# Scores of a slot's query chunks as one TensorE task, and smaller bookings in the ordering pass

## The chip, the cores and the metric

The kernel runs on one core of one Trainium2 chip. The metric is the device time of one execution in microseconds (us). An execution of the kernel before takes 1092.42 us (median of 3 runs).

## What is computed

Four batches of eight heads, 576 tokens, 64 dimensions each: causal softmax attention mixed with a linear memory read-out, and behind it two feed-forward layers on the 2304 x 512 result. All is float32.

```python
scores = where(causal, -1e9, q @ k.T / 8);  a = softmax(scores)
local  = a @ v
q_p    = where(q > 0, q, exp(q) - 1) + 1
mem    = (q_p @ M_prev) / (q_p @ z_prev + 1e-6)
x      = g * mem + (1 - g) * local            # g = sigmoid(beta), by head
h      = x @ moe_w_in;   x = (h * tanh(softplus(h))) @ moe_w_out
h      = x @ moe2_w_in;  out = (h * cos(h)) @ moe2_w_out
```

## The kernel before

**Attention.** `pair(m)` (L346) handles two heads of one batch; there are 16 pairs. It loads q, k, v, transposes q and k on TensorE (`prep`, L387: `f_tr` issues two or three transposes into one PSUM buffer, tiles ptq and ptk, and `f_ev` copies them to qT and kT). The 576 queries are five chunks, 0 of 64 rows and 1 to 4 of 128. They are dealt to three slots, `SLOTS = ((3, 0), (4,), (2, 1))`: slots 0 and 2 hold two chunks, slot 1 holds one. For each chunk `slot(x)` (L460) issues

- `f_sc` (L484): the scores of both heads into the slot's PSUM tile s (L491, two matmuls of 64 rows each), and the causal mask added by bf16 matmuls of pick and mask (L495); for chunk 4 also `f_sx` (L499, tile sx);
- `f_mx` (L513): the negated row maximum on VectorE (tile nm, L516), one column pair of nm for each chunk of the slot;
- `f_ex` (L528): the exponentials on ScalarE, one for each head, which read s and nm and write p (L532);
- `f_ph` (L544): the memory columns of p; and for the whole slot the sums and `f_sl` (L567), which scales p on VectorE (L569).

`flip` (L588) transposes p on TensorE (L584, tile t) and copies the blocks to PT; `pv` (L635) multiplies PT with v and M_prev (L651), the result goes through xs to DRAM.

**First feed-forward layer, first half.** `block0(bi)` (L718) takes 256 tokens at a time as soon as the four pairs of their batch are in DRAM: x is loaded and split in two float parts (x <- x, L731), `f_1` (L750, matmul line L756, tile h) and `f_2` (L791, matmul line L799, tile acc) are tasks of six matmuls. There are 9 such blocks, 1728 matmuls, and they lie between and behind the attention work. The weights are decoded on VectorE and ScalarE by `decode_w` (tiles dec and w, L125 to L142). The second half of the layer and the second layer (`late`, L884, L964, L966) follow.

**What sets the order.** All of this is first only booked: `add(engine, cost, function, deps, rank, takes, uses)` notes a task with a cost in us. `arrange()` (L176) then plays the tasks on a clock of its own: an engine that is free takes the ready task of lowest rank and is busy for the booked cost, buffers come free when all their users have ended, and TensorE is charged `SWITCH` when the mode of its tiles changes. The result is one list, and `run` issues the instructions in that order; each engine executes its own instructions in exactly that order. The booked costs therefore set the order alone. Where TensorE finds nothing ready before the first block0 task and its booked work of the last moments is too little, `arrange` inserts a dummy matmul (L303, tile warm) booked with 0.12 us (L250 to L260).

In the list as issued, a task's waits follow from what tiles its instructions read and write in the order of the list. So a matmul that writes s behind an instruction that reads s waits for that reader.

Of the kernel before, what the change touches and what calls it, by code (L numbers as in the profile page):

```python
# [10 lines left out]
F32 = mybir.dt.float32  # L11
# [18 lines left out]
def tile_kernel(ctx: ExitStack, tc: tile.TileContext, q, k, v, M_prev, z_prev, beta,  # L30
                moe_w_in, moe_w_out, moe2_w_in, moe2_w_out, out):
    nc = tc.nc
    B, H, S, D = q.shape
    NT, DM = out.shape
    DFF = moe_w_in.shape[1]
    P = 128
# [60 lines left out]
    pools = {}  # L97
# [243 lines left out]
    def misc(name):  # L341
        return pools["misc"].tile([P, 512], F32, tag="m", name=name)
# [3 lines left out]
    def pair(m):  # L346
# [40 lines left out]
        def prep(key, x):  # L387
            group = (QG if key == "q" else KG)[x]
            at = (0, 320 if key == "q" else 288)[x]
            w = sum(r for c, r in group)  # L390
            bm = Buf("misc")
            s = {}

            def f_tr(e):
                s["ps"] = ps = misc(f"pt{key}{m}_{x}")
                o = 0
                for c, r in group:
                    nc.tensor.transpose(ps[:, o:o + r], d[key][0:r, c].rearrange("p h d -> p (h d)"), ident[0:r, 0:r])  # L398
                    o += r

            def f_ev(e):
                if x == 0:
                    d[key + "T"] = A2.tile([P, S], F32, tag=f"{key}T", name=f"{key}T{m}")
                copy(e, d[key + "T"][:, at:at + w], s["ps"][:, 0:w], 0.125 if key == "q" else None)


            def f_kd(e):
                t = d["kd"] = kd[m % 2]
                for j in range(2):
                    copy(e, t[j * D:(j + 1) * D, j], s["ps"][j * D:(j + 1) * D, 512 - at:S - at])  # L410

            T_ = B_[key + "T"]
            takes = [bm] + ([T_] if x == 0 else []) + ([B_["kd"]] if key == "k" and x else [])
            tr = add("pe", 0.11 * len(group) + 0.05, f_tr, [dk if key == "k" else dq], R + 6, takes, [B_[key]])
            ev = add("act/dve", c_both(w), f_ev, [tr], R + 6, [], [bm, T_])
            got[key, x] = [ev]
            if key == "k" and x == 1:
                got[key, x].append(add("act/dve", (0.5, 0.4), f_kd, [tr], R + 6, [], [bm, B_["kd"]]))
# [41 lines left out]
        def slot(x):  # L460
# [1 line left out]
            bx = Buf("misc") if 4 in SLOTS[x] else None  # L462
            s = {"sp": {}}
            S_ = R + 20 + 10 * x
            at = 0
            def f_pt():
                if "pt" in s:
                    return
# [5 lines left out]
                    d["p", i_] = t[:, o:o + 2 * n_ + P].rearrange("p (h c) -> p h c", h=2)  # L474
                    o += 2 * n_ + P

            maxes, exps, cols = [], {}, {}
            t_m = fst = None
            for c, i in enumerate(SLOTS[x]):
                s0, nk = START[i], START[i] + ROWS[i]  # L480
                main = min(nk, 512)


                def f_sc(e, c=c, i=i, s0=s0, nk=nk, main=main, at=at):  # L484
                    if c == 0:
                        s["sc"] = pools["sc"].tile([P, 2, 512], F32, tag="s", name=f"s{m}_{x}")
                    o = s["sp"][i] = s["sc"][:, :, at:at + main]
                    qT, kT = d["qT"], d["kT"]
                    for j in range(2):
                        pr = slice(j * D, (j + 1) * D)  # L490
                        nc.tensor.matmul(o[:, j], qT[pr, s0:s0 + P], kT[pr, 0:main], start=True, stop=False)  # L491
                    for y in range(2 if i else 1):
                        for j in range(2):
                            pr = slice(j * D, (j + 1) * D)
                            nc.tensor.matmul(o[:, j, s0:main], pick[pr, y], mask[pr, y, 0:main - s0],  # L495
                                             start=False, stop=y == 1 or i == 0)


                def f_sx(e, s0=s0):  # L499
                    f_pt()  # L500
                    s["sx"] = o = misc(f"sx{m}")[:, 0:P]
                    nc.tensor.matmul(o, d["qT"][:, s0:s0 + P], d["kd"].rearrange("p j c -> p (j c)"), start=True, stop=False)
                    nc.tensor.matmul(o, ident_b, mask2.rearrange("p j c -> p (j c)"), start=False, stop=True)

                qd = [*got["q", 0 if i < 3 else 1]]
                kx = [*got["k", 0], *(got["k", 1] if nk > SH else ())]
                t_s = add("pe", main * 4 / 2400 + 0.35, f_sc, qd + kx + maxes[-1:], S_, [bs] if c == 0 else [],
                          [B_["qT"], B_["kT"]] + ([] if c == 0 else [bs]), mode=1)
                maxes.append(t_s)
                if nk > 512:  # L510
                    t_x = add("pe", 0.35, f_sx, qd + kx + maxes[-1:], S_, [bx, bp], [B_["qT"], B_["kd"]])

                def f_mx(e, c=c, i=i):  # L513
                    if c == 0:
                        s["nm"] = A2.tile([P, 2, 2], F32, tag="nm", name=f"nm{m}_{x}")
                    nc.vector.tensor_reduce(out=s["nm"][:, c], in_=s["sp"][i], axis=AX.X, op=ALU.max, negate=True)  # L516

                def f_mxx(e):
                    nm = s["nm"]
                    nc.vector.tensor_reduce(out=nm[:, 1], in_=s["sx"].rearrange("p (j c) -> p j c", j=2), axis=AX.X,  # L520
                                            op=ALU.max, negate=True)
                    nc.vector.tensor_tensor(out=nm[:, 0], in0=nm[:, 0], in1=nm[:, 1], op=ALU.min)

                t_m = add("dve", c_dve(2 * main), f_mx, [t_s, t_m], S_ + 1, [bn] if c == 0 else [], [bs] if c == 0 else [bs, bn])
                if nk > 512:
                    t_m = add("dve", 0.45, f_mxx, [t_m, t_x], S_ + 1, [], [bx, bn])

                def f_ex(e, j, part, c=c, i=i, main=main, nk=nk):  # L528
                    f_pt()
                    lo, hi = ((0, main), (main, nk))[part]  # L530
                    src = s["sp"][i][:, j] if part == 0 else s["sx"][:, j * HD:(j + 1) * HD]
                    nc.scalar.activation(d["p", i][:, j, D + lo:D + hi], src, AF.Exp, bias=s["nm"][:, c, j:j + 1], scale=1.0,  # L532
                                         accum_out=s["sm"][:, 1 if part else c, j:j + 1])

                for part in range(2 if nk > 512 else 1):
                    for j in range(2):
                        w = (main, nk - main)[part]
                        takes = [] if fst or bx else [bp]
                        t_e = add("act", 0.48 + 0.00083 * w, lambda e, j=j, part=part, f=f_ex: f(e, j, part), [t_m, fst], S_ + 2,
                                  takes, [bn] + ([] if takes else [bp]) + [bs if part == 0 else bx], func="exp")  # L540
                        exps[i, j, part] = t_e
                        fst = fst or t_e

                def f_ph(e, i=i):  # L544
                    nc.vector.tensor_tensor(out=d["p", i][:, :, 0:D], in0=d["ph"][:, i],  # L545
                                            in1=d["den"][:, i].unsqueeze(2).broadcast_to([P, 2, D]), op=ALU.mult)

                cols[i] = add("dve", 0.27, f_ph, [p4, fst], S_ + 3, [], [bp, B_["ph"], bden])
                at += nk

            def f_sm(e):
                sm = s["sm"]
# [35 lines left out]
        def flip(i, blocks, dst, x):  # L588
            nonlocal f0
            bm = Buf("misc")  # L590
            s = {}
            n = sum(ROWS[i_] for i_, h, j in blocks)

            def f_t(e):
                s["ps"] = ps = misc(f"t{m}_{i}")
                o = 0
                for i_, h, j in blocks:
                    tr(ps, o, i_, h, j)
                    o += ROWS[i_]

            def f_e(e):
                if "PT" not in d:
                    d["PT"] = A1.tile([P, 30, P], F32, tag="PT", name=f"PT{m}")
                o = dst(d["PT"])
                src = s["ps"][:, 0:n]
                if len(o.shape) == 3:
                    src = src.rearrange("p (a c) -> p a c", c=o.shape[2])
                copy(e, o, src)

            S_ = R + 25 + 10 * x  # L610
            t_t = add("pe", 0.115 * len(blocks) + 0.05, f_t, [f0] + [z_ for i_, h, j in blocks for z_ in (scaled[i_, h], colsof[i_])],
                      S_, [bm] + ([] if f0 else [B_["PT"]]), [ptof[i_] for i_, h, j in blocks])
            f0 = f0 or t_t
            t_e = add("act/dve", c_both(n), f_e, [t_t], S_ + 1, [], [bm, B_["PT"]])
            for i_, h, j in blocks:
                flipped.setdefault(i_, []).append(t_e)
# [510 lines left out]
```

## Time and profile before

| | us |
|---|---|
| time, median of 3 runs (lowest, highest) | 1092.42 (1090.91, 1093.68) |
| the profiled execution: its own time | 1091.78 |
| the profiled execution: span of its instructions | 1090.0 |
| TensorE (PE) busy | 1056.5 |
| VectorE (DVE) busy | 761.1 |
| ScalarE (ACT) busy | 570.6 |

The profile is one execution of the program. Its own time is 1.78 us longer than the span of its instructions. A group of instructions is named by its line, its engine, its operation, and the tiles it writes and reads (`nm<-s`). Idle time is that of the engine just ahead of the instruction, with what released it. Busy time of TensorE counts overlapping matmuls once, while the mean of one instruction is its full duration, so the time that one of a series costs is busy time divided by their number.

### The profile page before, as it was taken

Reading aid. Unit: us, or ns where it says so; the run is one execution under the profiler, and the core shown is the slowest. Engines: PE = TensorE matmul, PEld = TensorE weight load, DVE = VectorE, ACT = ScalarE, POOL = GpSimd, SP = SyncE. Lnnn points to the kernel's source line nnn. Section 1 sums busy time; section 2 is a strip of 40 time slices with the busy share of each in tenths; the row PEclk is TensorE's granted clock in tenths of the full one; section 3 lists DMA queues with packets and bytes.
Section 4 is the critical chain, followed back from the end, with each engine's and each line's share of the span. In section 5 each row is a group of like instructions: output and inputs, shape, how many; then the busy total and the mean of one; then the engine's idle time right before and its main releaser. Section 6 shows DMA issues by size and latency. Waiting matters only on the chain.

```text
span 1090.0 us, 17872 instructions
## 1 busy us (share of the span) xinstructions
PE 1056.5 (97%) x6907; PEld 937.7 (86%) x6907; DVE 761.1 (70%) x1699; ACT 570.6 (52%) x1272; POOL 3.9 (0%) x19
## 2 busy tenths in 40 slices
PE   7888999999999999999999999999999999999998
PEld 5555777877877899989999999999999999999997
DVE  6999997878768577537562218887667676666664
ACT  4666676756665433333323224766555455555544
POOL 1000000000000000000000000000000000000000
PEclk9999999999999999999999999999999999999999
DMA  6456322422230445306452215311000010000000
GB/s 158 108 150 170 92 64 67 120 65 59 69 105 25 161 146 161 120 25 205 166 184 87 72 44 174 117 39 59 1 29 30 1 59 1 29 30 1 30 1 29
DMA packets 112852, 88.71 MB, mean 81 GB/s; under 512 B 65792, under 2 KB 103680, under 8 KB 112768
## 3 DMA queue, kind: packets, MB, share of 16 engines
q1 hardware_dynamic: 112768, 87.58, 26.9%
q8 instruction: 54, 0.88, 0.3%
q14 instruction: 30, 0.25, 0.1%
HBM read 68.69 MB, written 18.87 MB: 80 GB/s over the span
## 4 chain that ended last, share of the span: by engine, by line
PE 85%; DVE 10%; ACT 3%; issue 1%; POOL 0%; ACTq 0%; POOLq 0%
PE h L884 28%; PE acc L966 18%; PE acc L964 9%; PE h L756 9%; PE acc L799 8%; PE pv L651 4%; PE t L584 4%; DVE nm L516 3%; PE s L491 3%; DVE p L569 2%; ACT p L532 1%; PE ptq L398 1%; DVE PT L317 1%; PE warm L303 1%; DVE p L545 1%
## 5 line engine op out<-in xcount | busy, mean ns | idle before, releaser
L884 PE MATMUL h<-x,w 128*128 128x384 f32 x1728 | 345.0, 337 | 1.6 <-ACT g L900 1.6
L884 PEld LDWEIGHTS h<-x,w 128*128 128x128 f32 x1728 | 307.3, 188 | 17.2 <-ACT g L900 1.8
L966 PE MATMUL acc<-w,G 128*128 128x512 f32 x864 | 228.4, 393 | 0.0
L966 PEld LDWEIGHTS acc<-w,G 128*128 128x128 f32 x864 | 159.9, 188 | 22.1
L951 DVE TENSOR_TENSOR G<-g,G 128x384 fp32r<-128x384 f32 x144 | 79.7, 555 | 100.1 <-ACT G L315 99.5
L756 PE MATMUL h<-x,w 128*128 128x256 f32 x864 | 128.9, 288 | 2.7 <-ACT g L315 1.6
L799 PE MATMUL acc<-G,w 128*128 128x256 f32 x864 | 129.9, 289 | 1.0 <-ACT o L315 0.7
L756 PEld LDWEIGHTS h<-x,w 128*128 128x128 f32 x864 | 111.6, 190 | 6.9 <-ACT g L315 4.5
L315 ACT ACTIVATE G<-g 128x384 fp32r<-128x384 f32 (+1 forms) x153 | 81.9, 535 | 66.3 <-DVE g L935 35.5
L799 PEld LDWEIGHTS acc<-G,w 128*128 128x128 f32 x864 | 112.2, 190 | 3.8 <-ACT o L315 1.9
L964 PE MATMUL acc<-G,w 128*128 128x384 f32 x576 | 112.6, 336 | 0.0
L532 ACT ACTIVATE p<-s,nm 128x448 f32<-128x448 f32 (+4 forms) x160 | 81.4, 517 | 43.7 <-DVE nm L516 16.4
L964 PEld LDWEIGHTS acc<-G,w 128*128 128x128 f32 x576 | 100.9, 188 | 0.0
L584 PE MATMUL t<-ident,p 128*128 128x128 f32 (+1 forms) x480 | 74.1, 280 | 10.5 <-DVE PT L317 6.3
L928 ACT ACTIVATE n<-n 128x384 f32<-128x384 f32 x96 | 49.9, 521 | 63.8 <-DVE n L924 63.8
L900 ACT ACTIVATE g<-h 128x384 f32<-128x384 f32 x48 | 23.5, 492 | 113.6 <-PE h L884 112.7
L516 DVE TENSOR_REDUCE nm<-s 128x2 f32<-128x128 f32 (+4 forms) x80 | 62.4, 793 | 21.8 <-PE s L495 11.2
L912 DVE TENSOR_SCALAR u<-hs 128x384 f32<-128x384 f32 x96 | 34.5, 359 | 54.6 <-ACT hs L315 51.9
L935 DVE TENSOR_TENSOR g<-n,hs 128x384 f32<-128x384 f32 x96 | 53.2, 555 | 26.3 <-ACT n L931 26.2
L584 PEld LDWEIGHTS t<-ident,p 128*128 128x128 f32 (+1 forms) x480 | 53.3, 142 | 21.2 <-DVE PT L317 8.8
L491 PE MATMUL s<-kT,qT 64*128 64x512 f32 (+4 forms) x320 | 61.8, 472 | 9.6 <-DVE nm L516 5.9
L315 ACT ACTIVATE hs<-h 128x384 f32<-128x384 f32 x96 | 47.1, 490 | 39.2 <-PE h L884 36.5
(91 smaller groups left out, 1216.4 us busy)
## 6 DMA issues: line engine op xcount, KB each, us to landing
raw<-in_moe_w_in_dram SPq DMA_DIRECT2D x32, 512.0 KB, 4.3
raw<-in_moe_w_out_dram SPq DMA_DIRECT2D x32, 512.0 KB, 4.0
k<-in_k_dram SPq DMA_DIRECT2D x32, 144.0 KB, 2.8
x1d<-xs SPq DMA_DIRECT2D x32, 144.0 KB, 2.0
xad<-o SPq DMA_DIRECT2D x9, 512.0 KB, 3.0
x2d<-o SPq DMA_DIRECT2D x6, 768.0 KB, 3.2
x<-x2d SPq DMA_DIRECT2D x6, 768.0 KB, 4.3
out_dram<-o SPq DMA_DIRECT2D x18, 256.0 KB, 2.0
```

The costliest lines, as they stand in the source:

```text
L315: nc.scalar.activation(dst, src, AF.Copy, scale=1.0 if scale is None else scale)
L491: nc.tensor.matmul(o[:, j], qT[pr, s0:s0 + P], kT[pr, 0:main], start=True, stop=False)
L516: nc.vector.tensor_reduce(out=s["nm"][:, c], in_=s["sp"][i], axis=AX.X, op=ALU.max, negate=True)
L532: nc.scalar.activation(d["p", i][:, j, D + lo:D + hi], src, AF.Exp, bias=s["nm"][:, c, j:j + 1], scale=1.0, accum_out=s["sm"][:, 1 if part ...
L584: nc.tensor.transpose(ps[:, at:at + r], d["p", i][0:r, h, j * P:(j + 1) * P], ident[0:r, 0:r])
L756: nc.tensor.matmul(h[:, half // 2], w[:, a, 0, c * P:(c + 1) * P], x[:, e_, c, :], start=c == 0 and pi == 0, stop=c == NKC - 1 and pi == 2)
L799: nc.tensor.matmul(t[:, c], w[:, a, 1, n * P:(n + 1) * P], G[:, e_, half], start=f == 0 and pi == 0 and c == 0, stop=f == NFH - 1 and pi == 2,
L884: nc.tensor.matmul(q_["h"], w[:, a, 0, c * P:(c + 1) * P], x[:, e_, c, :], start=c == 0 and pi == 0, stop=c == NKC - 1 and pi == 2)
L935: nc.vector.tensor_tensor(out=q_["g"], in0=q_["n"], in1=q_["hs"], op=ALU.mult)
L951: ENG[e].tensor_tensor(out=q_["G"][:, 1], in0=q_["g"], in1=q_["G"][:, 0].bitcast(F32), op=ALU.subtract)
L964: nc.tensor.matmul(o, w[:, a, 1, c * P:(c + 1) * P], G[:, e_, :], start=st, stop=sp_)
L966: nc.tensor.matmul(o, G[:, a, c * P:(c + 1) * P], w[:, e_, 1, :], start=st, stop=sp_)
```

## The change

`f_sc` moves out of the loop over the slot's chunks: it issues the scores and masks of all chunks of the slot behind each other, and is one task. It waits for both halves of kT and for every half of qT that its chunks need. Its booking is `main * 4 / 2400 + 0.15` for each chunk, where each chunk was a task of its own with `main * 4 / 2400 + 0.35`. The bookings of the transposes shrink: of q and k from `0.11 * n + 0.05` to `0.1 * n + 0.02`, of p from `0.115 * n + 0.05` to `0.109 * n + 0.02`. The second transpose task of q or k depends on the first one, and the tiles qT and kT are allocated with the first transposes instead of with the first copy.

```diff
             def f_tr(e):
+                if x == 0:
+                    d[key + "T"] = A2.tile([P, S], F32, tag=f"{key}T", name=f"{key}T{m}")
                 s["ps"] = ps = misc(f"pt{key}{m}_{x}")
...
-            tr = add("pe", 0.11 * len(group) + 0.05, f_tr, [dk if key == "k" else dq], R + 6, takes, [B_[key]])
+            tr = add("pe", 0.1 * len(group) + 0.02, f_tr, [dk if key == "k" else dq, *got.get((key, "tr"), ())], R + 6, takes, [B_[key]])
+            got[key, "tr"] = [tr]
...
-                def f_sc(e, c=c, i=i, s0=s0, nk=nk, main=main, at=at):
-                    if c == 0:
-                        s["sc"] = pools["sc"].tile([P, 2, 512], F32, tag="s", name=f"s{m}_{x}")
+            def f_sc(e):
+                s["sc"] = pools["sc"].tile([P, 2, 512], F32, tag="s", name=f"s{m}_{x}")
+                qT, kT = d["qT"], d["kT"]
+                at = 0
+                for i in SLOTS[x]:
+                    s0, main = START[i], min(START[i] + ROWS[i], 512)
                     o = s["sp"][i] = s["sc"][:, :, at:at + main]
...
+            t_s = add("pe", sum(min(START[i] + ROWS[i], 512) * 4 / 2400 + 0.15 for i in SLOTS[x]), f_sc, qd + kx, S_, [bs],
+                      [B_["qT"], B_["kT"]], mode=1)
...
-                t_s = add("pe", main * 4 / 2400 + 0.35, f_sc, qd + kx + maxes[-1:], S_, [bs] if c == 0 else [],
-                          [B_["qT"], B_["kT"]] + ([] if c == 0 else [bs]), mode=1)
-                maxes.append(t_s)
                 if nk > 512:
-                    t_x = add("pe", 0.35, f_sx, qd + kx + maxes[-1:], S_, [bx, bp], [B_["qT"], B_["kd"]])
+                    t_x = add("pe", 0.35, f_sx, [*qd, *kx, t_s], S_, [bx, bp], [B_["qT"], B_["kd"]])
...
-            t_t = add("pe", 0.115 * len(blocks) + 0.05, f_t, [f0] + [z_ for i_, h, j in blocks for z_ in (scaled[i_, h], colsof[i_])],
+            t_t = add("pe", 0.109 * len(blocks) + 0.02, f_t, [f0] + [z_ for i_, h, j in blocks for z_ in (scaled[i_, h], colsof[i_])],
```

How the change moves instructions, at three places. In tile names the first number is the pair and the second the slot or the part; most lines of the changed program stand three to nine lines further down.

**TensorE, slot 2 of pair 14, where block0 tasks fill the engine.** Before (the bf16 weight loads and masks are left out):

```order
L799 MATMUL acc0_3_0_3994<-G0_3_3_4295,w0_6_1744 128x256 x6
L756 MATMUL h0_4_1_4388<-x4_3711,w0_2_1001 128x256 x6
L491 MATMUL s14_2_4415<-kT14_4050,qT14_4191 128x320 x2
...
L799 MATMUL acc0_3_0_3994<-G0_3_3_4295,w0_7_1919 128x256 x6
L491 MATMUL s14_2_4415<-kT14_4050,qT14_4191 128x192 x2
...
L584 MATMUL t14_3_4445<-ident_85,p14_0_4337 128x128 x4
```

Now:

```order
L759 MATMUL h0_4_1_4175<-x4_3886,w0_3_1262 128x256 x6
L491 MATMUL s14_2_4501<-kT14_4081,qT14_4282 128x320 x2
...
L491 MATMUL s14_2_4501<-kT14_4081,qT14_4282 128x192 x2
...
L587 MATMUL t14_3_4521<-ident_85,p14_0_4456 128x128 x4
L759 MATMUL h0_4_2_4530<-x4_3886,w0_4_1445 128x256 x12
```

The scores of the second chunk (192 columns) stood behind another task and now follow those of the first (320 columns) with only their masks between.

**TensorE, the end of pair 4 and the first block0 matmuls (h0_0_0).** Before (dummies left out where the dots are):

```order
L584 MATMUL t4_4_1456<-ident_85,p4_1_1336 128x128 x4
L584 MATMUL t4_4_1464<-ident_85,p4_1_1336 128x128 x4
...
L584 MATMUL t4_4_1478<-ident_85,p4_1_1336 128x128 x2
L756 MATMUL h0_0_0_1482<-x0_1325,w0_0_452 128x256 x6
```

Now:

```order
L587 MATMUL t4_4_1487<-ident_85,p4_1_1317 128x128 x4
L587 MATMUL t4_4_1494<-ident_85,p4_1_1317 128x128 x4
L587 MATMUL t4_4_1505<-ident_85,p4_1_1317 128x128 x2
L587 MATMUL t4_2_1511<-ident_85,p4_2_1424 128x128 x3
L587 MATMUL t4_2_1516<-ident_85,p4_2_1424 128x128 x3
...
L759 MATMUL h0_0_0_1536<-x0_1373,w0_0_444 128x256 x6
L587 MATMUL t4_1_1546<-ident_85,p4_2_1424 128x128 x2
```

Six transposes of slot 2 (t4_2), and further up the first transposes of q of pair 5 and of k of pair 6, now stand ahead of the first block0 matmul: 12 more transposes in all. The dummies ahead of it are 218 instead of 187.

**VectorE, the row maxima of slots 0 and 1 of pair 4.** Before:

```order
L128 SCALAR_TENSOR_TENSOR dec0_4_1_1257<-raw0_4_1_1063,dec0_4_1_1257 128x512
L516 TENSOR_REDUCE nm4_0_1318<-s4_0_1296 128x2
L516 TENSOR_REDUCE nm4_1_1331<-s4_1_1311 128x2
L516 TENSOR_REDUCE nm4_0_1318<-s4_0_1296 128x2
L545 TENSOR_TENSOR p4_0_1333<-ph4_1259,den4_1292 128x2x64 x2
```

Now:

```order
L520 TENSOR_REDUCE nm4_0_1306<-s4_0_1183 128x2
L142 TENSOR_TENSOR w0_3_1262<-dec0_3_1_1241,w0_3_1262 128x512
L438 TENSOR_TENSOR mn4_1271<-ph4_1300,z4_1020 128x640
L520 TENSOR_REDUCE nm4_0_1306<-s4_0_1183 128x2
L444 TENSOR_REDUCE den4_1336<-mn4_1271 128x10
```

Between the two maxima of slot 0 stood one instruction and now stand two. The second one still comes behind exponentials of the first chunk: it writes the tile nm which they read, and waits for the last of them that is ahead of it in the list, before for that of the first head, now for that of the second.

**Counts over the whole order.** From the first block0 matmul to the last one TensorE changes between the modes of its tiles (scores; p times V; all else) 112 times before and 96 times now. Ahead of the last matmul of the attention stand 834 of the 1728 block0 matmuls before and 942 now. Ahead of the first split of x on VectorE (x <- x, L731) there are now three decode steps, three copies to PT and two copies to kT fewer, and two copies to qT, four to kd, four scalings of p, two small sums and one copy to xs more.

## Rows read from the trace of the kernel before

**Rows 1.** The page: busy time of the engines.

```profile
PE 1056.5 (97%) x6907; PEld 937.7 (86%) x6907; DVE 761.1 (70%) x1699; ACT 570.6 (52%) x1272; POOL 3.9 (0%) x19
```

**Rows 2.** Busy time by stretch: from, to, length, engines, clock, DMA.

```profile
0.00:107.00 107.00, 89.72 (x720) 61.67 (x721) 93.82 (x246) 63.92 (x200) 3.87 (x19) 0.98 0.56 145
107.00:360.00 253.00, 244.37 (x2052) 196.54 (x2052) 206.69 (x540) 165.74 (x445) 0.00 (x0) 1.00 0.29 74
360.00:500.00 140.00, 135.95 (x1060) 130.97 (x1059) 84.57 (x153) 55.00 (x86) 0.00 (x0) 1.00 0.44 142
500.00:1090.00 590.00, 586.48 (x3081) 548.55 (x3079) 376.05 (x764) 285.97 (x542) 0.00 (x0) 1.00 0.17 59
```

**Rows 3.** Timeline of TensorE around the first matmul of block0.

```profile
106.88 0.44 PE L584 MATMUL t<-ident,p 128*128 128x128 f32 x2
107.07 0.96 PE L756 MATMUL h<-x,w 128*128 128x256 f32 x6
```

**Rows 4.** Waits of TensorE from 107 to 360 us: total, times, longest.

```profile
PE s L491 <- DVE nm L516: 4.5, 8, 1.6
PE s L491 <- ACT p L532: 1.1, 3, 0.5
PE ptk L398 <- DVE kT L317: 0.8, 1, 0.8
PE h L756 <- DVE g L317: 0.8, 1, 0.8
```

**Rows 5.** TensorE groups by form from 107 to 360 us, the scores.

```profile
L491 PE MATMUL s<-kT,qT 64*128 64x192 f32 x44 | 6.6, 375 | 3.4 <-DVE nm L516 2.5 <-ACT p L532 0.8
L491 PE MATMUL s<-kT,qT 64*128 64x64 f32 x44 | 4.8, 295 | 2.5 <-DVE nm L516 2.0 <-ACT p L532 0.4
```

**Rows 6.** TensorE groups from 0 to 107 us: dummies and transposes.

```profile
L303 PE MATMUL warm<-zeros,ident_b 128*128 128x256 bf16 x187 | 28.5, 293 | 2.0 <-DVE zeros L300 2.0
L584 PE MATMUL t<-ident,p 128*128 128x128 f32 (+1 forms) x139 | 23.3, 293 | 9.8 <-DVE PT L317 6.0 <-ACT PT L315 2.0 <-ACT kd L315 1.5
```

**Rows 7.** VectorE groups by form, whole span: those of the count.

```profile
L131 DVE SCALAR_TENSOR_TENSOR dec<-raw,dec 128x512 int32<-128x512 int32 x64 | 43.9, 687 | 1.0
L317 DVE COPY PT<-t 128x512 f32<-128x512 f32 x32 | 21.8, 684 | 1.1 <-PE t L584 0.8
L569 DVE TENSOR_SCALAR p<-p,sm 128x320 f32<-128x320 f32 x32 | 11.0, 380 | 0.1
L319 DVE TENSOR_SCALAR qT<-ptq 128x320 f32<-128x320 f32 x5 | 2.4, 482 | 0.1
L317 DVE COPY kd<-ptk 64x64 f32<-64x64 f32 x12 | 2.6, 217 | 0.1
```

**Rows 8.** Waits of VectorE from 20 to 107 us: total, times, longest.

```profile
DVE nm L516 <- ACT p L532: 1.3, 3, 0.9
DVE nm L516 <- PE s L495: 0.5, 2, 0.3
```

**Rows 9.** The same from 107 to 360 us.

```profile
DVE nm L516 <- ACT p L532: 8.2, 10, 2.0
```

**Rows 10.** Timeline of TensorE, scores of slots 0 and 1, and slot 2.

```profile
113.30 0.44 PE L491 MATMUL s<-kT,qT 64*128 64x64 f32 x4 [0.73 <-DVE nm L516]
...
113.60 1.11 PE L491 MATMUL s<-kT,qT 64*128 64x512 f32 x4
...
121.13 0.60 PE L491 MATMUL s<-kT,qT 64*128 64x192 f32 x4
...
121.77 2.41 PE L756 MATMUL h<-x,w 128*128 128x256 f32 x18
```

**Rows 11.** L799 alone by form: first 140 to 360 us, then 380 to 480 us.

```profile
L799 PE MATMUL acc<-G,w 128*128 128x256 f32 x354 | 56.1, 294 | 0.0
L799 PE MATMUL acc<-G,w 128*128 128x256 f32 x389 | 57.2, 284 | 0.4 <-DVE G L776 0.4
```

More of the change, by code (lines that the diff above doesn't have):

```diff
@@ L401, in f_ev @@
             def f_ev(e):
-                if x == 0:
-                    d[key + "T"] = A2.tile([P, S], F32, tag=f"{key}T", name=f"{key}T{m}")
                 copy(e, d[key + "T"][:, at:at + w], s["ps"][:, 0:w], 0.125 if key == "q" else None)
@@ L464, in slot @@
             S_ = R + 20 + 10 * x
-            at = 0
             def f_pt():
@@ L475, in f_pt @@
                     o += 2 * n_ + P
-            maxes, exps, cols = [], {}, {}
+            exps, cols = {}, {}
             t_m = fst = None
-            for c, i in enumerate(SLOTS[x]):
-                s0, nk = START[i], START[i] + ROWS[i]
-                main = min(nk, 512)
-                def f_sc(e, c=c, i=i, s0=s0, nk=nk, main=main, at=at):
-                    if c == 0:
-                        s["sc"] = pools["sc"].tile([P, 2, 512], F32, tag="s", name=f"s{m}_{x}")
+            def f_sc(e):
[4 more added lines that the diff above has]
+                    s0, main = START[i], min(START[i] + ROWS[i], 512)
                     o = s["sp"][i] = s["sc"][:, :, at:at + main]
-                    qT, kT = d["qT"], d["kT"]
                     for j in range(2):
@@ L496, in f_sc @@
                                              start=False, stop=y == 1 or i == 0)
+                    at += main
+            qd = [t_ for y in sorted({0 if i < 3 else 1 for i in SLOTS[x]}) for t_ in got["q", y]]
+            kx = [*got["k", 0], *got["k", 1]]
+            t_s = add("pe", sum(min(START[i] + ROWS[i], 512) * 4 / 2400 + 0.15 for i in SLOTS[x]), f_sc, qd + kx, S_, [bs],
+                      [B_["qT"], B_["kT"]], mode=1)
+            for c, i in enumerate(SLOTS[x]):
+                s0, nk = START[i], START[i] + ROWS[i]
+                main = min(nk, 512)
                 def f_sx(e, s0=s0):
@@ L503, in f_sx @@
                     nc.tensor.matmul(o, ident_b, mask2.rearrange("p j c -> p (j c)"), start=False, stop=True)
-                qd = [*got["q", 0 if i < 3 else 1]]
-                kx = [*got["k", 0], *(got["k", 1] if nk > SH else ())]
-                t_s = add("pe", main * 4 / 2400 + 0.35, f_sc, qd + kx + maxes[-1:], S_, [bs] if c == 0 else [],
-                          [B_["qT"], B_["kT"]] + ([] if c == 0 else [bs]), mode=1)
-                maxes.append(t_s)
                 if nk > 512:
-                    t_x = add("pe", 0.35, f_sx, qd + kx + maxes[-1:], S_, [bx, bp], [B_["qT"], B_["kd"]])
+                    t_x = add("pe", 0.35, f_sx, [*qd, *kx, t_s], S_, [bx, bp], [B_["qT"], B_["kd"]])
                 def f_mx(e, c=c, i=i):
@@ L548, in slot @@
                 cols[i] = add("dve", 0.27, f_ph, [p4, fst], S_ + 3, [], [bp, B_["ph"], bden])
-                at += nk
             def f_sm(e):
```

## The prediction

> **What bounds the kernel now.** I read the page first, then the busy time by stretch, then the waits inside the stretches that have idle time. TensorE is busy for 1056.5 of 1090.0 us [rows 1], so no other engine can be the bound over the whole span; but 28.5 us of that are dummies [rows 6]. Useful work of TensorE is 1056.5 - 28.5 = 1028 us, and the span is this plus dummies plus idle time. The stretches say where these lie [rows 2]. Up to 107 us TensorE is busy for 89.7 us, dummies among them, so 61.2 us are useful and 45.8 us are lost; VectorE is busy for 93.8 of the same 107 us. This start is bound by VectorE, and it ends with the first matmul of block0 at 107.07 us [rows 3], from which on TensorE always has feed-forward work beside the attention. From 107 to 360 us TensorE idles for 253.0 - 244.4 = 8.6 us, from 360 to 500 us for 4.0 us, and behind that for 3.5 us in 590 [rows 2]. So a change to the order can win in two ways only: by more useful matmuls in the start or a shorter start, and by less waiting behind it. From 500 us on there is nothing to win.
>
> Of the 8.6 us, 4.5 are scores that wait for the row maximum on VectorE and 1.1 are scores that wait for the exponentials on ScalarE [rows 4]. The forms name them: all of it lies ahead of the scores of 192 and of 64 columns [rows 5], which are the second chunks of slots 2 and 0. They write the tile s behind an instruction that reads its first part, and wait for that reader.
>
> **The change part by part.** The sum is made against the profiled execution's own time, 1091.78 us, which lies 0.64 below the median of 1092.42.
>
> *The wait of second chunks.* Now nothing reads s between the two chunks, so the wait goes by construction. TensorE bounds the time behind 107 us, so I count it all: 11 waits, **-5.6** [rows 4]. The same waits ahead of 107 us cost nothing, since TensorE has dummies and idle time there.
>
> *The transposes.* Twelve more stand ahead of the first block0 matmul. One costs 23.3 us / 139 = 0.168 us [rows 6], together **-2.0**: they fill time that is lost today, and are gone from the full stretch. The 31 further dummies lie in the same lost time and cost nothing as long as VectorE is the later engine there; if it weren't, they would cost 31 x 28.5/187 = 4.7 us [rows 6].
>
> *VectorE ahead of the first split of x.* Three decode steps and three copies to PT fewer at 0.68 to 0.69 us each, and two copies to kT that I price like the copy to qT, are -5.1 us. Two copies to qT at 0.48, four to kd at 0.22, four scalings at 0.38 and a copy to xs at about 0.5 are +3.9, two small sums some +0.2 [rows 7]. So the work of the engine that bounds the start hardly changes: **-1.0**.
>
> *The second maximum of a slot.* It waits for an exponential of the first chunk, since both touch nm. Now it often stands closer to the first maximum and waits for the exponential of the second head. In the start VectorE lost 1.3 us to that in 3 waits, 0.9 the longest [rows 8]. There are ten such places ahead of the first block0 matmul (five pairs, two slots). The bounds of what is added are 0 and 10 x 0.9 - 1.3 = 7.7; I take as much again as there is now, **+1.3**, as only 3 of 10 showed at all.
>
> *The first maximum of a slot.* It now waits for the scores of both chunks. A second chunk takes 113.60 - 113.30 = 0.30 us in slot 0 and 121.77 - 121.13 = 0.64 in slot 2 [rows 10], so five pairs give at most 5 x 0.94 = 4.7 us in the start, and at least 0. VectorE waited for scores for only 0.5 us from 20 to 107 us [rows 8]: it is usually late for them. I take **+0.5**. Behind 107 us VectorE has 253.0 - 206.7 = 46 us to spare [rows 2], and the delay is hidden as long as TensorE doesn't come to wait for VectorE in turn.
>
> *Mode changes.* There are 16 fewer. A block0 matmul costs 56.1/354 = 0.158 us between attention work and 57.2/389 = 0.147 by itself [rows 11], so a task of six loses 0.07 us to its neighbours. Sixteen of these are 1.1 us; not all of the loss is due to modes, so the bounds are -1.1 and 0, and I take **-0.6**. The Trainium skill, "TensorEngine Tiling (Array Packing)", Tiling Modes, says that a change of the tiling mode, not of the tile alone, drains the engine; by that all of the 0.07 would be the mode's, and the term would be -1.1.
>
> *New waits of TensorE behind 107 us.* The order is another one, with 108 more block0 matmuls among the attention. Everything but the second chunks idles TensorE for 8.6 - 5.6 = 3.0 us there now, mostly copies that a transpose or a block waits for [rows 4]. What is added lies between 0 and 5.6, the whole of what went; I take half of today's other waits, **+1.4**.
>
> Bookings themselves execute nothing. The other queues: SP issues the same loads, and the load of x for block0 stands behind the same stores as before.
>
> Sum: 1091.8 - 5.6 - 2.0 - 1.0 + 1.3 + 0.5 - 0.6 + 1.4 = 1085.8; with the 0.6 to the median, **1086.4 us**, 0.55% less. Without the three additions and with the full mode term it is 1082.7; if the other 3.0 us of waits went too, 1079.7. With all additions at their upper ends it is 1085.8 + (7.7 - 1.3) + (4.7 - 0.5) + (5.6 - 1.4) + 0.6 + 0.6 = 1101.8, but that is three bad ends at once.
>
> **Rivals.** *The waits come back elsewhere.* TensorE reaches the next transposes or the next slot's scores 5.6 us sooner and finds VectorE or ScalarE no sooner. Then the last term is 5.6 instead of 1.4, and the time 1090.6. For it: in-order VectorE already loses 8.2 us to ScalarE at second maxima in that stretch, 2.0 the longest [rows 9]. Against it: its 46 us to spare, and that with the block0 tasks that now stand between, TensorE rarely meets a result that is not ready.
>
> *The first maxima become late in the start.* If in the start the scores were always the later ones, that term is 4.7 instead of 0.5: also 1090.6. Rows show a matmul of a second chunk held up for 0.73 us by the maximum of the first [rows 10], so the two exclude each other in time already, the other way round. The Trainium skill, "PSUM — Partial Sum Buffer", PSUM bank collisions raise a hardware error, tells to guard PSUM by bank and not by address, which fits that row; by it no finer wait than that for the whole task is to be had where the chunks share a bank. Against this rival stands the 0.5 us of [rows 8].
>
> *Slower: the second maxima stretch the start.* Its place is VectorE ahead of the first block0 matmul, where every us counts. In pair 4 only two instructions stand between the two maxima of slot 0 now, while ScalarE has evictions and two exponentials to do; with a mean wait w at ten places the time is 1086.4 - 2.6 + 10w. It is slower by over 0.3% (1095.7) from w = 1.2 us on, and with the longest wait of the later stretch, 2.0 us [rows 9], it is 1103.8. Against it: today's mean is 1.3/10 = 0.13 us, the longest 0.9 [rows 8].
>
> **How the numbers follow.** 0.3% (3.3 us) is about what a measurement of this kernel can tell from no change. My forecast, below 1089.1, has a chance of 0.57. The two rivals that give 1090.6 have 0.16 and 0.09; together 0.25 for no measurable change. The slower rival has 0.18: the start has 45.8 us of loss to grow from, and the new order there was read but not timed. The range reaches from 1079, where all small terms fall well, to 1096, which takes in the two rivals and the beginning of the slower one; most of the slower one and a little below 1079 are left out.
>
> **What would show it.** Right: no idle time ahead of scores of 64 and 192 columns; TensorE's idle time between the first block0 matmul and 500 us falls from 12.6 to about 8; the first block0 matmul starts at 106 to 109 us with about 63 us of useful matmuls ahead of it. Wrong: a first block0 matmul behind 112 us with VectorE waiting for ScalarE at the maxima (the slower rival) or for scores (the second one); or transposes and copies that idle TensorE for over 7 us behind it (the first).

## The result and the profile after

The change takes 1081.82 us (median of 4 runs, 1081.23 to 1082.68) against 1092.39 us before (4 runs): the ratio is 0.9906, 95% interval 0.9893 to 0.9918. It gains 10.6 us, where 6.0 were forecast. The profiled execution has a span of 1080.1 us instead of 1090.0. Part of the gain goes with TensorE's granted clock: three of the change's four executions have a mean of 1.000 and take 1081.2 to 1081.9 us. Of 37 executions of the kernel before that ran beside the experiments below, three have 1.000, and these take 1090.8 to 1091.0 us. At equal clock the gain is 9.0 us, and the other 1.5 us are an estimate of the clock's part.

The page of the change, busy time of the engines:

```profile
PE 1053.2 (98%) x6938; PEld 938.7 (87%) x6938; DVE 761.6 (71%) x1694; ACT 570.1 (53%) x1279; POOL 3.8 (0%) x19
```

Busy time by stretch, cut at the first block0 matmul, which now starts at 105.84 us (columns as in [rows 2]; the last row takes in all that lies behind the cut):

```profile
0.00:105.84 105.84, 92.49 (x764) 64.61 (x765) 92.82 (x251) 65.96 (x205) 3.84 (x19) 1.00 0.55 142
105.84:360.00 254.16, 247.64 (x2112) 203.71 (x2113) 208.76 (x525) 167.11 (x447) 0.00 (x0) 1.00 0.29 78
360.00:500.00 140.00, 136.52 (x1042) 131.68 (x1042) 89.23 (x165) 54.67 (x93) 0.00 (x0) 1.00 0.46 147
...
105.84:1080.10 974.26, 960.75 (x6174) 874.09 (x6174) 668.76 (x1445) 504.18 (x1076) 0.00 (x0) 1.00 0.24 76
```

The same cut in the trace before, all that lies behind 107.07 us:

```profile
107.07:1090.00 982.93, 966.74 (x6188) 876.00 (x6187) 667.24 (x1454) 506.64 (x1073) 0.00 (x0) 1.00 0.24 74
```

The span is the sum of three parts: the time lost in the start (dummies and idle time up to the cut), all useful busy time of TensorE, and its idle time behind the cut. The dummies of the change take this long:

```profile
L303 PE MATMUL warm<-zeros,ident_b 128*128 128x256 bf16 x218 | 31.1, 285 | 2.0 <-DVE zeros L300 2.0
```

| us | before | change | difference |
|---|---|---|---|
| start up to the first block0 matmul | 107.1 | 105.8 | -1.2 |
| lost in the start (length less useful busy time) | 45.8 | 44.5 | -1.3 |
| useful busy time, start | 61.3 | 61.4 | 0.0 |
| useful busy time, behind | 966.7 | 960.8 | -6.0 |
| idle, behind | 16.2 | 13.5 | -2.7 |
| span | 1090.0 | 1080.1 | -9.9 |

Most of the gain is neither a shorter start nor less waiting: it stands as less useful busy time behind the cut. Some 2 us of that are transposes that moved ahead of the cut; the rest is work that takes less time. The waits, from the cut to 360 us (who waits for whom, total, times, longest):

```profile
PE h L759 <- DVE g L317: 3.5, 6, 1.0
PE pv L654 <- DVE PT L317: 1.3, 1, 1.3
PE s L491 <- ACT p L536: 1.1, 1, 1.1
PE t L587 <- ACT PT L315: 0.2, 1, 0.2
```

and the forms of the second chunks, which in [rows 5] carried 5.9 us of idle time, and the first chunk of slot 2:

```profile
L491 PE MATMUL s<-kT,qT 64*128 64x320 f32 x44 | 8.9, 481 | 1.1 <-ACT p L536 1.1
L491 PE MATMUL s<-kT,qT 64*128 64x192 f32 x44 | 6.0, 350 | 0.0
L491 PE MATMUL s<-kT,qT 64*128 64x64 f32 x44 | 4.4, 273 | 0.0
```

The waits of second chunks are gone without rest. In their place h, the PSUM buffer of block0, waits for its eviction on VectorE (the copy from h to g that frees the buffer), which cost 0.8 us before [rows 4]. The waits of VectorE in the start (20 to 105.84 us) are those of [rows 8], no more:

```profile
DVE nm L520 <- ACT p L536: 1.3, 4, 0.4
...
DVE nm L520 <- PE s L495: 0.6, 1, 0.6
```

### The profile page after: what moved, and what is told of

It is laid out like the page before. It is cut to its first block, busy times and chain, and to the rows that moved or that the text cites. A ratio compares the mean times of both kernels' runs of the same rounds, so it can differ in the third digit from the quotient of the medians.

```text
span 1080.1 us, 17930 instructions
## 1 busy us (share of the span) xinstructions
PE 1053.2 (98%) x6938; PEld 938.7 (87%) x6938; DVE 761.6 (71%) x1694; ACT 570.1 (53%) x1279; POOL 3.8 (0%) x19
## 4 chain that ended last, share of the span: by engine, by line
PE 88%; DVE 7%; ACT 3%; issue 1%; POOL 0%; ACTq 0%; POOLq 0%; DVEq 0%
PE h L887 28%; PE acc L969 18%; PE acc L967 9%; PE h L759 9%; PE acc L802 9%; PE pv L654 5%; PE t L587 4%; PE s L491 3%; DVE nm L520 2%; DVE p L572 1%; PE warm L303 1%; ACT p L536 1%; PE ptq L400 1%; ACT PT L315 1%; PE ptk L400 1%
## 5 line engine op out<-in xcount | busy, mean ns | idle before, releaser
L536 ACT ACTIVATE p<-s,nm 128x64 f32<-128x64 f32 (+4 forms) x160 | 81.3, 515 | 40.0 <-DVE nm L520 26.2
L931 ACT ACTIVATE n<-n 128x384 f32<-128x384 f32 x96 | 49.9, 521 | 63.5 <-DVE n L927 63.5
L520 DVE TENSOR_REDUCE nm<-s 128x2 f32<-128x1024 f32 (+4 forms) x80 | 62.2, 790 | 23.5 <-PE s L495 16.4
L315 ACT ACTIVATE PT<-t 128x256 f32<-128x256 f32 (+3 forms) x97 | 43.4, 466 | 42.0 <-PE t L587 41.5
```

The costliest lines, as they stand in the source:

```text
L315: nc.scalar.activation(dst, src, AF.Copy, scale=1.0 if scale is None else scale)
```

## The experiments

Twelve kernels ran beside the two: ten stand in the table, and two more, no_dummies and act_h_fix, are told below. The edits are shortened, with conditions put in words. The spans are taken apart like the change's; times are medians, ratios are to the kernel before on the same chip, with 95% intervals. "FF" is the number of block0 matmuls that stand ahead of the attention's last one, "modes" the mode changes of TensorE behind the first block0 matmul, counted by kind of task (scores; p times V; all else); both are read from the order. The three columns in the middle are worked out from the profiled execution.

| kernel | us | ratio | lost in start | useful busy | idle behind | modes | FF |
|---|---|---|---|---|---|---|---|
| before | 1092.4 | | 45.8 | 1028.0 | 16.2 | 112 | 834 |
| the change | 1081.8 | 0.9906 (0.9893 to 0.9918) | 44.5 | 1022.1 | 13.5 | 96 | 942 |
| adjacent | 1086.4 | 0.9943 (0.9922 to 0.9964) | 45.4 | 1025.0 | 15.1 | 88 | 834 |
| split | 1088.7 | 0.9965 (0.9952 to 0.9977) | 44.5 | 1025.6 | 15.8 | 124 | 942 |
| group_only | 1087.2 | 0.9953 (0.9937 to 0.9970) | 45.7 | 1024.1 | 15.2 | 89 | 846 |
| book_only | 1102.3 | 1.0090 (1.0071 to 1.0109) | 47.6 | 1032.3 | 22.0 | 113 | 1044 |
| tr_only | 1101.1 | 1.0073 (1.0054 to 1.0091) | 48.9 | 1032.3 | 18.8 | 119 | 912 |
| tr_old | 1088.2 | 0.9957 (0.9942 to 0.9972) | 46.5 | 1023.4 | 14.9 | 89 | 900 |
| sc35 | 1080.6 | 0.9888 (0.9873 to 0.9903) | 45.2 | 1021.0 | 13.4 | 82 | 942 |
| tr_less | 1089.1 | 0.9964 (0.9952 to 0.9976) | 49.9 | 1020.3 | 17.4 | 86 | 984 |
| tr_true | 1088.8 | 0.9962 (0.9948 to 0.9977) | 44.3 | 1026.2 | 16.3 | 89 | 810 |
| ff_true | 1089.8 | 0.9973 (0.9963 to 0.9983) | 45.1 | 1025.9 | 16.8 | 91 | 858 |

### Grouping by itself: adjacent

The order of before is kept; only the second chunk is pulled up.

```diff
     def run(order):
         for t in order:
+            if t is the score task of a second chunk: continue
             t.fn(t.on)
+            if t is the score task of a first chunk: issue that of the second
```

> The bookings and the order of the kernel before, but the scores of a slot's second chunk are issued directly behind those of its first; nothing else moves. TensorE changes its tile mode 88 instead of 112 times behind the first block0 matmul. Theory (the change gains by the chunks standing together): the 5.6 us of waits go, and 24 mode changes at 0.12 to 0.25 us each are 2.9 to 6.0 us more, so 1081 to 1084 us, about all that the change gained. Rival (the gain is the new order, above all the 108 block0 matmuls that the new bookings put among the attention): less than half of the 10.6 us, 1087 to 1092 us.

It took 1086.4 us: 5.9 us gained, between the two. Of the waits of [rows 4], the first two are gone, and others have grown (106.4 to 360 us):

```profile
PE t L600 <- DVE PT L332: 1.5, 4, 0.5
PE h L772 <- DVE g L332: 1.3, 1, 1.3
PE t L600 <- ACT PT L330: 1.3, 3, 0.6
PE ptk L413 <- DVE kT L332: 1.1, 1, 1.1
```

So 5.6 us of waits went and the idle time behind the cut fell by 1.1 us only: TensorE comes sooner to transposes and blocks whose inputs come no sooner. In the same order, the waits come back for the most part. The other part of this gain is busy time:

```profile
106.40:1085.50 979.10, 964.02 (x6188) 875.42 (x6187) 666.24 (x1454) 505.44 (x1073) 0.00 (x0) 1.00 0.24 75
```

964.0 instead of 966.7 us behind the cut, with the same matmuls: 2.7 us for 24 mode changes fewer, 0.11 us each.

### The price of a mode change: split

```diff
     # in the order of the change, T the TensorE task ahead of a two-chunk score task
-    T; scores of both chunks
+    scores of the first chunk; T; scores of the second chunk
```

> The order of the change, but behind the first block0 matmul the task ahead of a two-chunk score task, where it is of the ordinary tile mode, is issued between its two chunks. The second chunk stands ahead of the reader of the first in the list, so no wait comes with it: 124 instead of 96 mode changes, nothing else. Theory (a mode change costs TensorE time of its own, 0.12 to 0.25 us): 28 changes, 3.4 to 7 us slower than the change's 1081.8, so 1085.2 to 1088.8 us. Rival (only the waits cost, a mode change 0.04 us as in the prediction's term): 1081.8 to 1083 us.

It took 1088.7 us, 6.9 more than the change. The start is the same to 0.1 us; the useful time behind it is 964.2 instead of 960.8 us, 3.5 us for 28 mode changes, 0.12 us each; idle time rose by 2.3 us.

```profile
105.84:1085.90 980.06, 964.22 (x6174) 874.78 (x6174) 668.62 (x1445) 504.26 (x1076) 0.00 (x0) 1.00 0.25 75
```

The timeline of the change around one such place, and that of this kernel:

```profile
118.34 0.81 PE L491 MATMUL s<-kT,qT 64*128 64x320 f32 x4
118.98 0.28 PE L495 MATMUL s<-mask,pick 64*128 64x128 bf16 x4
119.09 0.55 PE L491 MATMUL s<-kT,qT 64*128 64x192 f32 x4
119.47 0.28 PE L495 MATMUL s<-mask,pick 64*128 64x128 bf16 x4
119.59 0.59 PE L400 MATMUL ptq<-ident,q 64*128 64x64 f32 x3
```

```profile
117.60 0.81 PE L518 MATMUL s<-kT,qT 64*128 64x320 f32 x4
118.24 0.28 PE L522 MATMUL s<-mask,pick 64*128 64x128 bf16 x4
118.45 0.97 PE L787 MATMUL h<-x,w 128*128 128x256 f32 x6
119.35 0.60 PE L518 MATMUL s<-kT,qT 64*128 64x192 f32 x4
119.78 0.28 PE L522 MATMUL s<-mask,pick 64*128 64x128 bf16 x4
```

In the change, the scores of 192 columns start 0.11 us behind the start of the last masks (118.98 to 119.09). In split, what follows a group of masks starts 0.21 us behind their start (118.24 to 118.45): the 0.1 us is the change of mode, and none of it shows as idle time. The change's own rows also show what counts as one: the transposes of 64 rows (ptq at 119.59) start 0.12 us behind the masks at 119.47, like scores. They have the scores' tile shape, 64*128, so nothing changes, though the column "modes" counts a change there.

Counted by the tile shapes in the traces, from the first block0 matmul to the last, there are 154 changes before, 133 with the change, 130 in adjacent and 155 in split. That is 24 fewer for 2.7 us (0.11 us each) and 22 more for 3.5 us (0.16 us each). In single pairs of matmuls of these four traces, the step from a last mask of 128 columns to the next matmul has a median of 0.05 us to scores and of 0.15 us to another shape. The step from a block0 matmul is 0.12 us to a matmul of its own shape and 0.21 us to scores. So a change by itself takes 0.09 to 0.10 us each way, and what split costs beyond that is not taken apart further. The Trainium skill, "TensorEngine Tiling (Array Packing)", Tiling Modes, says that such a change drains the engine; by that rule it costs time each time, and both runs agree.

### Grouping and bookings apart: group_only, book_only, tr_only, tr_old, sc35

```diff
 # group_only: the change with the old bookings
-            ... * 4 / 2400 + 0.15 ...   0.1 * len(group) + 0.02    0.109 * len(blocks) + 0.02
+            ... * 4 / 2400 + 0.35 ...   0.11 * len(group) + 0.05   0.115 * len(blocks) + 0.05
```

> The change with the bookings of before (0.35 us for each chunk, the larger transposes); the planner makes an order of its own, with 846 block0 matmuls ahead of the attention's end (834 before, 942 with the change) and 89 mode changes. Theory (grouping): 1082 to 1085 us. Rival (bookings): 1088 to 1092 us.

1087.2 us: 5.1 gained. That lies between the two ranges, 2.2 us above the grouping theory's and 0.8 us below the rival's, so neither holds as it stands: grouping with the old bookings has about half of the gain.

```diff
 # book_only: the kernel before with the smaller bookings
-            main * 4 / 2400 + 0.35    0.11 * len(group) + 0.05   0.115 * len(blocks) + 0.05
+            main * 4 / 2400 + 0.15    0.1 * len(group) + 0.02    0.109 * len(blocks) + 0.02
```

> The kernel before with the smaller bookings alone: a chunk is still a task, booked 0.2 us less, and the transposes less; 1044 block0 matmuls stand ahead of the attention's end, 113 mode changes. Theory (grouping): the waits of second chunks stay at 4 to 7 us, and what is gained is the start alone, 1087 to 1092 us. Rival (bookings): 1080 to 1085 us.

1102.3 us, ten slower than before. Neither had that. The three parts all grew, most of all the idle time behind the start (22.0 instead of 16.2 us), and the first block0 matmul came at 114.9 us.

```diff
 # tr_old: the change with the transposes' bookings of before
-            0.1 * len(group) + 0.02    0.109 * len(blocks) + 0.02
+            0.11 * len(group) + 0.05   0.115 * len(blocks) + 0.05
```

> The change with the transposes' bookings of before and the new booking of the scores. Its order has 399 attention matmuls ahead of the first block0 matmul (427 with the change, 430 with grouping and all old bookings), 89 mode changes, 900 block0 matmuls ahead of the attention's end. If the smaller bookings of the transposes carry what grouping alone (1087.2 us) lacks, this is 1085 to 1089 us; if the smaller booking of the scores carries it, 1081 to 1083 us.

```diff
 # sc35: the change with the scores booked as before, 0.35 us a chunk
-            ... * 4 / 2400 + 0.15 ...
+            ... * 4 / 2400 + 0.35 ...
```

> The other half: grouping, the transposes' smaller bookings, and 0.35 us for each chunk as before. 454 attention matmuls ahead of the first block0 matmul, 82 mode changes, 942 block0 matmuls ahead of the attention's end. If the transposes' bookings carry the rest, 1081 to 1083 us; if the scores' do, 1085 to 1089 us. If both halves miss it or both have it, the two bookings do not add and what is left is the particular order that each set of numbers draws.

1088.2 and 1080.6 us. Among the grouped kernels the smaller booking of the scores gains nothing that shows, and the transposes' bookings carry what grouping alone lacks. So I tried these alone, ungrouped:

```diff
 # tr_only: the kernel before with the transposes' new bookings and order
-            0.11 * len(group) + 0.05   0.115 * len(blocks) + 0.05
+            0.1 * len(group) + 0.02    0.109 * len(blocks) + 0.02
```

> The kernel before with the smaller bookings of the transposes alone (and the fixed order of the two transposes of q or k that they need); the chunks' scores are tasks of their own, booked as before. 119 mode changes, 912 block0 matmuls ahead of the attention's end. If the 6 us that these bookings bring with grouping (1087.2 to 1080.6 us) are theirs alone, 1085 to 1088 us. If they are worth something only where the second chunk does not wait for its reader, 1090 to 1097 us, with 4 to 7 us of waits of scores for VectorE.

1101.1 us, slower still than expected. Its waits from the first block0 matmul to 360 us begin with

```profile
PE s L492 <- DVE nm L517: 3.3, 8, 1.2
PE h L757 <- DVE g L317: 3.3, 4, 1.5
```

The same numbers gain 6.6 us with grouping (group_only to sc35) and lose 8.5 without it (before to tr_only). The waits of scores for row maxima are 3.3 us here up to 360 us and 4.5 of the 18.8 us of idle time over all, no more than before, so they do not explain the loss: the useful time is 4.2 us longer and 3.1 more are lost in the start. Most of the longer useful time is the clock, by these stretches of tr_only (columns as in [rows 2]):

```profile
130.00:135.50 5.50, 3.52 (x26) 2.56 (x25) 5.05 (x14) 5.24 (x11) 0.00 (x0) 1.00 0.29 83
135.50:142.30 6.80, 6.80 (x31) 4.37 (x31) 4.29 (x11) 2.23 (x7) 0.00 (x0) 0.50 0.03 13
```

TensorE was busy for 3.52 of 5.50 us, then the granted clock was at its lower level for 6.8 us of full work. At the upper level that work would take about half, so some 3.4 of the 4.2 us are an estimate of its price. The other executions agree that this is a part only: two with a mean clock of 0.997 instead of 0.995 still take 1100.4 us. What makes the rest of that order worse is open.

### Do truer bookings help? tr_less, tr_true, ff_true

```diff
 # tr_less, tr_true: sc35 with other transposes; the lines show q and k, then p
-            0.1 * len(group) + 0.02    0.109 * len(blocks) + 0.02
+            0.09 * len(group)          0.1 * len(blocks)            # tr_less
+            0.16 * len(group) + 0.02   0.15 * len(blocks) + 0.02    # tr_true
 # ff_true: the change, f_1 and f_2 of block0
-            add("pe", 0.73, ...
+            add("pe", 0.89, ...
```

> Grouping, 0.35 us for each chunk, and transposes booked smaller still: 0.09 us each of q and k, 0.1 us each of p, nothing for the task. 984 block0 matmuls ahead of the attention's end. If smaller bookings gain because they put more feed-forward work among the attention, it is as fast as the 1080.6 us of the same kernel with the change's bookings or faster, 1078 to 1082 us. If each set of numbers only draws another order, it lies anywhere from 1080 to 1090 us.

> Grouping, 0.35 us for each chunk, and transposes booked as the trace has them, 0.16 us each of q and k and 0.15 us each of p, and 0.02 us for the task. 810 block0 matmuls ahead of the attention's end. If small bookings gain by putting more feed-forward work among the attention, this is the slowest of the grouped ones, 1087 to 1092 us. If nearness to the measured durations is what helps, 1078 to 1082 us.

> The change, with the tasks of six block0 matmuls booked at 0.89 us, as the trace has them, instead of 0.73 us. 858 block0 matmuls ahead of the attention's end. If true bookings let the planner see that TensorE is full, it plans fewer waits and this is 1078 to 1081 us; if less feed-forward work among the attention costs, 1084 to 1090 us.

1089.1, 1088.8 and 1089.8 us. Smaller bookings still are no better, true ones neither, and the number of block0 matmuls among the attention (984, 810, 858) does not order the times. Each set of numbers draws another order, and with it places where TensorE waits and its clock falls: the trace of tr_less has 0.50 from 201.3 to 208.1 us, behind 3.20 us of work in 5.30. All eight grouped orders lie below before, from 1080.6 to 1089.8 us, and the change's is one of the two best. Its ratio and that of sc35 (1080.6 us) have overlapping intervals and are not told apart.

### The dummies: no_dummies

```diff
     def f_dummy(e):
-        nc.tensor.matmul(warm["w"][:, 0], ident_b, warm["z"], start=True, stop=True)
+        pass
```

> The order of the change with its 218 dummies left out; nothing else moves. Theory (dummies lie in time that the start loses anyway, and only hold up the clock): the clock of the start falls below 1.00, useful matmuls of the start take longer, and as VectorE bounds the start the time is 0 to 4 us above the change's 1081.8. Rival (dummies hold up transposes that stand behind them): the start gets shorter, 1078 to 1081 us.

1085.8 us (ratio 0.9942, 0.9923 to 0.9962): 4.0 more than the change, just within the theory's range. By stretch:

```profile
0.00:20.00 20.00, 13.36 (x66) 7.82 (x66) 12.28 (x39) 9.58 (x29) 3.86 (x19) 1.00 0.73 183
20.00:40.00 20.00, 16.70 (x100) 9.94 (x100) 16.66 (x42) 10.75 (x31) 0.00 (x0) 0.74 0.43 111
40.00:60.00 20.00, 14.91 (x119) 9.74 (x117) 17.96 (x53) 12.03 (x43) 0.00 (x0) 0.91 0.36 90
60.00:80.00 20.00, 16.55 (x133) 10.35 (x129) 18.79 (x47) 14.00 (x44) 0.00 (x0) 1.00 0.58 143
80.00:109.70 29.70, 21.67 (x138) 14.70 (x138) 26.50 (x72) 19.11 (x59) 0.00 (x0) 0.77 0.56 151
```

The granted clock is at its lower level (1.2 GHz) for parts of three of the five stretches, where the change has 1.00 throughout. Without dummies TensorE is busy for 83.2 us of the start with the same useful matmuls that take 61.4 in the change, and the first block0 matmul comes at 109.7 instead of 105.8 us. VectorE then waits for TensorE too: it is busy for 16.7 of 20 us at the first fall, and for 18.6 in the change's stretch from 20 to 40 us:

```profile
20.00:40.00 20.00, 17.75 (x146) 11.59 (x147) 18.61 (x50) 12.98 (x39) 0.00 (x0) 1.00 0.46 117
```

The dummies do not hold up the start; they pay for themselves.

### Evictions of h on ScalarE: act_h_fix

```diff
         for t in order:
-            t.fn(t.on)
+            t.fn("act" if t is an eviction of h else t.on)
```

> The order of the change, but the 17 evictions of h that the planner gave to VectorE are done by ScalarE at the same places of the list. In the change h waits 3.5 us for these evictions between the first block0 matmul and 360 us, and 0.8 us behind it. If they wait because VectorE works its list off in order and comes to them late, this saves 2 to 4 us: 1078 to 1080 us. Rival (ScalarE is as late at those places, or its exponentials get late instead): 1081 to 1084 us.

1084.8 us (ratio 0.9929, 0.9912 to 0.9945), 3 slower than the change and 0.8 above the rival's range. The theory fails, and the rival's reason shows: ScalarE is as late at those places, and its longest wait is twice as long. But that is a small part of the 3 us: the profiled execution, the only one of the four with a mean granted clock of 1.000, takes 1082.4 us, while the others have 0.998 and take 1084.7 to 1085.2 us. Whether the edit lowered their clock is open.

```profile
PE h L759 <- ACT g L315: 4.5, 6, 2.2
PE pv L654 <- DVE PT L317: 1.3, 1, 1.3
```

## Why the prediction was right in its way and short in its size

The time lies within the range (1079 to 1096 us) and the forecast case, faster by over 0.3%, came true. But its sum had 6.0 us, and the runs show 10.6, or 9.0 at equal clock. Of its signs, idle time ahead of the second chunks is gone as forecast; TensorE's idle time to 500 us fell from 12.6 to 10.0 us instead of about 8, and the useful matmuls of the start took 61.4 us instead of about 63. By its steps:

- **The wait of second chunks, -5.6.** Right: no idle time is left ahead of those forms. **New waits, +1.4** was too small: idle time behind the start fell by 2.7 us, so 2.9 came in. In the order of before (adjacent) even 4.5 of 5.6 came back, most of what the first rival held. It was not fatal since busy time was gained beside it, which the sum had all but left out; that part of the good outcome is luck.
- **Mode changes, -0.6.** This step failed. I took what a block0 task loses among attention work, 0.07 us, for the price of a change, and halved it. But the 0.07 us is a mean over tasks: the 354 matmuls of [rows 11] are 59 tasks, and the same trace has only 28 changes of tile shape next to them. The same rows give 59 x 0.07 = 4.1 us for 28 changes, 0.15 us each if all of the loss is theirs. Measured by two opposite edits it is 0.11 and 0.12 us by the count of tasks, so 16 changes are 1.9 us, beyond the bound of 1.1 that I gave; by tile shape there are 21 fewer, and at the 0.09 to 0.11 us of single pairs and of adjacent they are 1.9 to 2.3 us.
- **Useful time behind the start** fell by 6.0 us in all: 2.0 are the 12 transposes now ahead of it (at 0.168 us), 1.9 the mode changes. The remaining 2 us are not explained by an experiment. Where they stand can be read: with each matmul of the two traces counted from the end of the one before, scores take 3.0 us less, sx 0.8 and the transposes 2.3, and no other kind moved by more than 0.2.
- **The transposes, -2.0, and VectorE's count, -1.0.** In line with them, the first block0 matmul comes 1.2 us sooner, with 12 more transposes ahead of it; no run parts the two. That the useful time of the start did not grow by 2 us fits the trace before, where the clock fell:

```profile
40.00:44.70 4.70, 3.20 (x25) 2.28 (x23) 4.60 (x14) 3.26 (x13) 0.00 (x0) 1.00 0.62 161
44.70:48.10 3.40, 3.08 (x15) 2.80 (x16) 3.29 (x9) 2.41 (x7) 0.00 (x0) 0.50 0.04 9
```

  Some of the useful matmuls there ran at the lower level; the change has 1.00 up to the cut. The sum had no term for this, and the 1.5 us between 10.6 and the 9.0 us at equal clock are an estimate of its size. That the change by itself keeps the clock up is not shown: act_h_fix has the same order on TensorE and a mean of 0.998 in three of four executions.
- **The two maxima, +1.3 and +0.5.** Neither came: VectorE's waits for exponentials in the start are 1.3 us as before, those for scores 0.6 instead of 0.5. The slower rival and the one of late first maxima rested on these waits and fell with them.
- **The dummies cost nothing.** Right, and more: without them the start is longer.
- **What the bookings do.** I wrote that they execute nothing and set the order alone, and priced the order's effect as small terms. Grouping, with the order of before, is 5.9 us; the other 4.7 us come with the particular order that the change's numbers draw. With the same bookings and no grouping the order is 10 us slower than before. My range would not have held that.

## What to carry to other kernels

Where an engine is full and switches between tile modes, put the matmuls of one mode together: here a change cost about 0.1 us that shows nowhere as idle time, only in the busy time of the same work. A wait that is taken from a full in-order engine is worth what the next wait leaves of it: in the same order 4.5 of 5.6 us came back. And with a planner, test an edit in a fixed order first: the orders that other bookings drew for the same edit spread over 9 us, and neither truer nor smaller bookings were better as a rule.

## What was not expected of the hardware

The clock of TensorE fell in the start although the engine was busy for most of it: without dummies, behind 13.4 us of work in the first 20, the granted clock was 0.74 from 20 to 40 us and 0.77 from 80 to 110 us, and the same useful matmuls took 83.2 instead of 61.4 us. And a change of tile mode does not appear as a gap: in the timeline, the next group starts 0.1 us later, under the modelled end of the last one.
